# A gated mix of a state-space scan and a long convolution: every fourth step scanned, 32 x 64 conv digits, and half of the output gated first

## The chip, the cores and the metric

The kernel runs on one core of one Trainium2 chip. The metric is the device time of one execution in microseconds; the runs shown are three executions of the kernel before. Engines are named as in the profile: PE (TensorE, matmuls), PEld (its weight loads), DVE (VectorE), ACT (ScalarE), POOL (GpSimd), SP (SyncE, which here only issues DMAs). The 16 DMA engines are counted together.

## What is computed

Two sequence models read the same x (2048 steps, 1024 channels, bf16) and a sigmoid gate mixes them, one gate per step.

```python
def _A_ref(x, Lambda_re, Lambda_im, B_re, B_im, C_re, C_im, log_dt, Dskip):
    ...
    Lam_bar = jnp.exp(dt * Lam)
    B_bar = ((Lam_bar - 1.0) / Lam)[:, None] * Bmat
    Bu = jnp.einsum("bld,pd->blp", x + 0j, B_bar)
    for t in range(L):
        h = Lam_bar[None, :] * h + Bu[:, t, :]
        hs.append(h)
    y = 2.0 * jnp.einsum("blp,dp->bld", hseq, Cmat).real + x * Dskip[None, None, :]

def _B_ref(q, k, v, shift_k, ssm_k, ssm_D):
    # k_shift: a causal filter of 4 taps over k, per channel
    kv = k_shift * v
    # y: the causal convolution of kv with ssm_k over all 2048 steps, per channel, by FFT
    y = y + kv * ssm_D[None, None, :]
    return q * y

g = _sigmoid((x * gate_w).sum(-1, keepdims=True))
return g * _A_ref(x, ...) + (1 - g) * _B_ref(x, B_k, B_v, ...)
```

There are 1024 complex states. Matmuls take bf16 and accumulate in fp32.

## The kernel before, in words

**The planner.** The kernel does not issue its work in program order. Every piece of work is given to a `_Plan` by `op` (L76): its engine, an assumed duration, the tiles that it reads and writes, and a priority. `schedule` (L114) then simulates the engines with these durations, with the buffers in SBUF (21 slabs of 8 KB per partition), eight PSUM banks in pairs and a serial DMA server, and fixes the order on each engine; `emit` (L294) writes the instructions in that order. The priorities are the tables PS, PU, PO, PC, PH, PG. A piece with an `alt` may go to a second engine: evacuations from PSUM (`evac`, L519) to ACT or DVE, many DMAs to SP's queue or POOL's. Each queue is in order, so a waiting instruction holds what stands behind it.

**S5, the scan (L836 on).** States are taken 128 at a time, in 8 groups `pi`. x is loaded transposed (`load_x`, L612) in four tiles `xT` of 512 steps: odd and even steps, first and second half. `gemm_u` (L875) multiplies B and x, re and im apart, 16 matmuls of 128x128 by 512 for each tile. For even steps it adds the product of the previous odd step with the transition (`prev`, L885), so that only every second step has to be scanned. `rot` (L905) turns the input by the phase of the transition, scans re and im with the real decay (L923), and turns back: four DVE products and sums on each side; it does so for two chunks of 512, with a carry computed on POOL. `odd` (L943) then computes the odd steps from the even ones with 6 matmuls. Four of the eight groups stay in SBUF, four go to the scratch `h_scr` and come back.

**The convolution (L701 on).** Channels are taken 128 at a time, in 8 groups `u`. `kvprep` (L716) loads k and v transposed, applies the four taps and multiplies by v on DVE (some on ACT), and writes the product to `kv_scr`; `load_A` (L702) reads it and the kernel rows back with the time axis over the partitions in 16 parts of 128. The transform has digits 16, 16 and 16: `stage1` (L742), 8 matmuls of 128 columns; `spec` (L753), for two of 16 frequencies a matmul of 512 columns and two of 256; `product` (L766), the complex product, a DVE product of 2048 (L772) and two sums of 512 (L776); `inverse` (L780), matmuls of 256 and 128 columns, an evacuation and four DMAs that move one digit across partitions into `zb`; and `final` (L795), 8 full matmuls of 512, a multiplication by x on DVE (L808) and a DMA to the scratch `pB_scr`.

**The output (L1085).** Sixteen blocks of 256 steps by 512 channels: for each half 16 matmuls of 512 columns over all eight state groups (L1125). The conv part is read from `pB_scr`, scaled by 1 - g on ACT (L1107), x times Dskip is added on DVE (L1099, L1113), and a DVE operation adds g times the matmul's result (L1134). A block needs all state groups and its rows of `pB_scr`. The C matrices are combined with the coefficients of B on ACT and DVE before (L1053 to L1065). The gate's sums are matmuls on four column tiles (`gates`, L958).

The lines that the prediction names: L510 to L520 are helpers (`dma`, `evac`), so all DMAs show as L513 (transposing) or L515, and all evacuations as L520.

Of the kernel before, what the change touches and what calls it, by code (L numbers as in the profile page):

```python
# [15 lines left out]
MAGIC = 12582912.0  # L16
# [3 lines left out]


# [9 lines left out]
class _Op:  # L31
    __slots__ = ("alt", "eng", "dur", "fn", "prio", "n", "succ", "tiles", "alloc", "ready", "start", "end", "dma", "idx")


class _Plan:
# [3 lines left out]
    SLAB = 8192  # L39

    def __init__(self, nslab, nps):
        self.ops = []
        self.tags = {}
        self.nslab, self.nps = nslab, nps
        self.nbig, self.horizon, self.bias = 4, 40.0, 0.0
        self.least, self.spare = {}, 0

    def tile(self, tag, shape, dtype=BF16, cap=2, hold=False, loose=False):
# [4 lines left out]
        size = 2048 if b <= 2048 else 4096 if b <= 4096 else 8192  # L53
        assert b <= 8192
# [21 lines left out]
    def op(self, eng, dur, fn, r=(), w=(), prio=0.0, dma=None, alt=None):  # L76
        o = _Op()
        o.alt = alt
# [27 lines left out]
        for p_ in preds:  # L106
            p_.succ.append(o)
        for t in o.tiles:
            t.touches += 1
# [4 lines left out]
    def schedule(self, free0):  # L114
# [5 lines left out]
        halves = [[None] * 4 for _ in range(self.nslab)]  # L120
# [13 lines left out]
        def find(size, loose):  # L134
            k = size // 2048
            best = None
            big = sum(left[tg] + live.get(tg, 0) for tg, c_ in caps.items() if c_[1] == 8192 and not c_[3])
            for s, h in enumerate(halves):
                if big and (s < self.nbig) != (size == 8192 and not loose):
                    continue  # L140
                used = 4 - h.count(None)
                for q in range(0, 4, k):
                    if all(x is None for x in h[q:q + k]):
                        pair = (h[q ^ 1] is not None) if k == 1 else False
                        sc = (pair, used)
                        if best is None or sc > best[0]:
                            best = (sc, s, q)
            return best and best[1:]

        def fits_after(t):  # L150
            big = sum(left[tg] + live.get(tg, 0) for tg, c_ in caps.items() if c_[1] == 8192 and not c_[3])
            lo = self.nbig if big else 0
            free = sum(h.count(None) for h in halves[lo:]) - t.size // 2048
            need = 0
            for tg, (cap, size, hold, loose) in caps.items():
                if size and not hold and not loose and (size < 8192 or not big):
                    need += max(0, min(self.least.get(tg, 1), cap) - live.get(tg, 0)) * size // 2048 if left[tg] else 0
            return free >= need + self.spare

        def take(o):  # L160
            got = []
            for t in o.tiles:
# [9 lines left out]
                else:  # L172
                    if t.order != nexta.get(t.tag, 0) or live.get(t.tag, 0) >= t.cap or (t.hold and not fits_after(t)):
                        break
# [46 lines left out]
        while True:  # L221
            progress = True
            while progress:
                progress = False
                for e in engs:
# [3 lines left out]
                    for o in cand:  # L229
# [14 lines left out]
                        if o.dma is None:  # L244
                            o.end = now + o.dur
                            efree[e] = o.end
# [71 lines left out]
def kernel(  # L318
# [31 lines left out]
    SE = S // 2  # L350
    CW = 512
    NC = SE // CW
# [3 lines left out]
    NG = CH // 8  # L356
# [6 lines left out]
    kv_scr = dram.tile([D, S], BF16, name="kv_scr")  # L363
    h_scr = dram.tile([NP, NC, 128, 4 * CW], BF16, name="h_scr")
    g_scr = dram.tile([2, SE], F32, name="g_scr")

# [5 lines left out]
    prow = parm.tile([32, 128], BF16, name="prow")  # L372
    for i, v1d in enumerate((A_log_dt, A_Lambda_re, A_Lambda_im, A_Dskip)):
# [5 lines left out]
    sdz = parm.tile([128, D // 8], BF16, name="sdz")  # L379
    nc.vector.memset(sdz, 0.0)  # L380
# [4 lines left out]
    nc.vector.memset(mpi_col, -math.pi)  # L385
    mpih_col = consts.tile([128, 1], F32, name="mpih_col")
# [4 lines left out]
    make_identity(nc, ident)  # L391
    psum = ctx.enter_context(tc.tile_pool(name="psum", bufs=1, space=bass.MemoryType.PSUM))
# [5 lines left out]
    nc.tensor.matmul(psums[0][:, 0:32], lhsT=prow, rhs=ident[0:32, 0:32], start=True, stop=True)  # L398
    pcol = parm.tile([128, 32], F32, name="pcol")
    nc.vector.tensor_copy(pcol, psums[0][:, 0:32])  # L400
# [6 lines left out]
    dco = parm.tile([128, NP, 3], F32, name="dco")  # L407
# [24 lines left out]
    r2 = small("r2")  # L432
    mul(r2, rv, rv)
# [13 lines left out]
    TS(out=phn, in0=thn, scalar1=2.0, scalar2=None, op0=ALU.mult)  # L447
    rc = dco[:, :, 0]
    mul(rc, rv, cth)
    rs = dco[:, :, 2]  # L450
    mul(rs, rv, sth)
    mrs = dco[:, :, 1]
    TS(out=mrs, in0=rs, scalar1=-1.0, scalar2=None, op0=ALU.mult)
# [17 lines left out]
    phU = small("phU")  # L471
    TS(out=phU, in0=phn, scalar1=float(CW), scalar2=None, op0=ALU.mult)
    rqU = small("rqU")
    TS(out=rqU, in0=phU, scalar1=MAGIC, scalar2=-MAGIC, op0=ALU.add, op1=ALU.add)
    TT(out=phU, in0=phU, in1=rqU, op=ALU.subtract)
    sU = small("sU")
    nc.scalar.activation(out=sU, in_=phU, func=ACT.Sin, scale=TWO_PI)
    faU = small("faU")
    nc.scalar.activation(out=faU, in_=phU, func=ACT.Abs)
    cU = small("cU")  # L480
    nc.scalar.activation(out=cU, in_=faU, func=ACT.Sin, bias=pihalf_col, scale=-TWO_PI)
    sU2 = parm.tile([128, NP, 2], F32, name="sU2")
    TS(out=sU2[:, :, 0], in0=sU, scalar1=-1.0, scalar2=None, op0=ALU.mult)
    nc.vector.tensor_copy(sU2[:, :, 1], sU)
# [3 lines left out]
    omgc = parm.tile([128, 16], F32, name="omgc")  # L488
# [702 lines left out]
```

## Time and profile before

| | us |
|---|---|
| median of three runs | 434.52 (430.0 to 436.05) |
| span of the profiled execution | 427.0 |
| PE busy | 398.4 (93%) |
| DVE busy | 346.7 (81%) |
| ACT busy | 267.8 (63%) |
| POOL busy | 132.7 (31%) |
| packets of SP's DMA queue, share of 16 engines' span | 69.8% |
| packets of POOL's DMA queue | 16.9% |

The profile gives the span, from the first to the last instruction of one execution, and no other time of that execution; 434.52 - 427.0 = 7.5 us lie around it against the median. The DMA queues moved 71.87 MB in 153,596 packets, 129,861 of them under 512 bytes. Matmuls are pipelined: the mean of one (379 ns for 512 columns) is its way through the array and not the distance to the next; distances are read from the chain or the timeline, where a run of them stands with its count. DMA shares are sums of packet times and can exceed 1.

### The profile page before, as it was taken

Reading aid. Unit: us, or ns where it says so; the run is one execution under the profiler, and the core shown is the slowest. Engines: PE = TensorE matmul, PEld = TensorE weight load, DVE = VectorE, ACT = ScalarE, POOL = GpSimd, SP = SyncE. Lnnn points to the kernel's source line nnn. Section 1 sums busy time; section 2 is a strip of 40 time slices with the busy share of each in tenths; the row PEclk is TensorE's granted clock in tenths of the full one; section 3 lists DMA queues with packets and bytes.
Section 4 is the critical chain, followed back from the end, with each engine's and each line's share of the span. In section 5 each row is a group of like instructions: output and inputs, shape, how many; then the busy total and the mean of one; then the engine's idle time right before and its main releaser. Section 6 shows DMA issues by size and latency. Waiting matters only on the chain.

```text
span 427.0 us, 7194 instructions
## 1 busy us (share of the span) xinstructions
PE 398.4 (93%) x2691; PEld 228.5 (54%) x2736; DVE 346.7 (81%) x513; ACT 267.8 (63%) x310; POOL 132.7 (31%) x172
## 2 busy tenths in 40 slices
PE   7598999999999789999969999899989999999996
PEld 6353544655566456566635655676544444444442
DVE  4998999999979789989889989979696969724422
ACT  3489488747589679477966786999554286203100
POOL 6994611232464134753634403340010000000000
PEclk9999999999999999999998999999999999999999
DMA  8999999459999999598999369999989996405111
GB/s 149 113 196 195 194 232 231 174 90 160 158 186 193 256 217 185 127 207 173 187 184 164 90 192 166 287 184 178 174 163 185 213 234 205 143 22 177 49 37 62
DMA packets 153596, 71.87 MB, mean 168 GB/s; under 512 B 129861, under 2 KB 147541, under 8 KB 153561
## 3 DMA queue, kind: packets, MB, share of 16 engines
q1 hardware_dynamic: 146120, 54.55, 69.8%
q0 software_dynamic: 7360, 16.85, 16.9%
q8 instruction: 21, 0.34, 0.4%
q14 instruction: 15, 0.11, 0.1%
q10 hardware_dynamic: 80, 0.01, 0.0%
HBM read 24.93 MB, written 16.79 MB: 98 GB/s over the span
## 4 chain that ended last, share of the span: by engine, by line
PE 68%; DMA 11%; SPq 10%; ACT 4%; DVE 3%; issue 3%; POOL 0%; DVEq 0%; ACTq 0%; POOLq 0%
PE ps L1125 22%; PE ps L882 20%; SPq L513 8%; DMA slab<-slab 5%; PE ps L760 4%; ACT slab L520 4%; PE ps L747 4%; DMA slab<-in_A_x_dram 4%; PE ps L889 3%; PE ps L950 3%; DMA slab<-in_B_ssm_k_dram 3%; PE ps L761 2%; PE ps L786 2%; PE ps L762 2%; SPq L515 2%
## 5 line engine op out<-in xcount | busy, mean ns | idle before, releaser
L520 ACT CAST slab<-ps 128x1024 bf16<-128x1024 f32 x197 | 185.4, 1042 | 62.8 <-PE ps L892 17.6
L882 PE MATMUL ps<-slab,slab 128*128 128x512 bf16 (+1 forms) x527 | 115.8, 370 | 6.3 <-DMA slab<-in_A_B_re_dram 3.1
L1125 PE MATMUL ps<-slab,slab 128*128 128x512 bf16 x485 | 109.1, 379 | 1.0 <-DVE slab L1134 0.4
L882 PEld LDWEIGHTS <-slab 128*128 128x128 bf16 x544 | 52.8, 99 | 60.0 <-issue 5.5
L1125 PEld LDWEIGHTS <-slab 128*128 128x128 bf16 x512 | 49.8, 98 | 59.6 <-issue 0.7
L515 POOL DMA_DIRECT2D slab<-slab x84 | 51.4, 618 | 57.8 <-ACT slab L520 51.9
L1134 DVE SCALAR_TENSOR_TENSOR slab<-ps,gcols,slab 128x512 bf16<-128x512 f32 x32 | 23.6, 747 | 39.1 <-PE ps L1125 36.1
L1107 ACT ACTIVATE slab<-slab,omgc 128x512 bf16<-128x512 bf16 x32 | 21.2, 714 | 45.2 <-DMA slab<-pB_scr 40.1
L760 PE MATMUL ps<-slab,fC 128*128 128x512 bf16 x118 | 44.9, 381 | 1.1 <-ACT slab L520 0.6
L747 PE MATMUL ps<-tab,slab 128*128 128x128 bf16 x512 | 35.0, 222 | 7.5 <-POOL slab L712 6.2
L911 DVE TENSOR_TENSOR slab<-slab,slab 128x2048 bf16<-128x2048 bf16 x31 | 37.7, 1217 | 3.5 <-PE ps L747 1.5
L772 DVE TENSOR_TENSOR slab<-slab 128x2048 bf16<-128x2048 bf16 x32 | 38.6, 1215 | 1.8 <-ACT slab L520 1.5
L747 PEld LDWEIGHTS <-slab 128*128 128x128 bf16 x512 | 31.4, 99 | 12.3 <-POOL slab L712 6.8
L761 PE MATMUL ps<-slab,fS 128*128 128x256 bf16 x128 | 35.0, 273 | 0.6 <-issue 0.2
L762 PE MATMUL ps<-slab,fN 128*128 128x256 bf16 x128 | 35.0, 274 | 0.0
L786 PE MATMUL ps<-slab,gC 128*128 128x256 bf16 x128 | 29.9, 273 | 1.7 <-DVE slab L776 1.7
L776 DVE TENSOR_TENSOR slab<-slab 128x512 bf16<-128x512 bf16 x64 | 24.9, 416 | 6.3 <-PE ps L950 2.3
L788 PE MATMUL ps<-slab,gS 128*128 128x128 bf16 x128 | 28.0, 219 | 0.0
L787 PE MATMUL ps<-slab,gN 128*128 128x128 bf16 x128 | 28.0, 219 | 0.0
L735 DVE TENSOR_TENSOR slab<-slab,slab 128x2047 bf16<-128x2047 bf16 (+2 forms) x22 | 26.7, 1213 | 0.0
L808 DVE TENSOR_TENSOR slab<-ps,slab 128x1024 bf16<-128x1024 f32 x16 | 19.3, 1216 | 3.3 <-PE ps L806 2.8
L1113 DVE SCALAR_TENSOR_TENSOR slab<-slab,gcols,slab 128x512 bf16<-128x512 bf16 x26 | 18.3, 745 | 3.5 <-ACT slab L1107 3.4
(184 smaller groups left out, 532.5 us busy)
## 6 DMA issues: line engine op xcount, KB each, us to landing
slab<-in_A_x_dram SPq DMA_DIRECT2D x22, 256.0 KB
slab<-slab POOLq DMA_DIRECT2D x84, 64.0 KB, 5.3
slab<-h_scr SPq DMA_DIRECT2D x8, 512.0 KB
slab<-pB_scr SPq DMA_DIRECT2D x16, 256.0 KB
out_dram<-slab SPq DMA_DIRECT2D x15, 256.0 KB
slab<-in_B_ssm_k_dram SPq DMA_DIRECT2D x7, 512.0 KB
pB_scr<-slab SPq DMA_DIRECT2D x12, 256.0 KB
slab<-slab SPq DMA_DIRECT2D x44, 64.0 KB
```

Of the source, the lines that this page charges most:

```text
L513: nc.sync.dma_start_transpose(out=o_, in_=i_)
L515: QS[q].dma_start(out=o_, in_=i_)
L520: op("ACT", 1.04, lambda: A.copy(o_(), i_()), r=r, w=w, prio=prio, alt=("DVE", 1.2, lambda: V.tensor_copy(o_(), i_())))
L747: PE_.matmul(ps.ap[:, i, :], lhsT=a.ap[:, 8 * q + i, :], rhs=t1v[:, hh * 128:(hh + 1) * 128], start=True, stop=True)
L760: PE_.matmul(ps.ap[:, i], lhsT=fC[:, k2, :], rhs=zz, start=True, stop=False)
L761: PE_.matmul(ps.ap[:, i, :, 0, :], lhsT=fS[:, k2, :], rhs=zz[:, :, 1, :], start=False, stop=False)
L762: PE_.matmul(ps.ap[:, i, :, 1, :], lhsT=fN[:, k2, :], rhs=zz[:, :, 0, :], start=False, stop=True)
L772: TT(out=T.ap, in0=K.unsqueeze(2).to_broadcast([128, 2, 2, 4 * CH]), in1=W_.unsqueeze(1).to_broadcast([128, 2, 2, 4 * CH]), op=ALU.mult)
L786: PE_.matmul(ps.ap[:, i], lhsT=gC[:, k2, :], rhs=pp.ap[:, :, i, :], start=True, stop=False)
L882: PE_.matmul(ps.ap[:, ri, k0:k1], lhsT=BT.ap[:, d, ri, :], rhs=t.ap[:, d, k0:k1], start=(d == 0), stop=(par == 1 and d == ND - 1))
L911: TT(out=out, in0=tab.ap.unsqueeze(2).to_broadcast([128, 2, 2, CW]), in1=x.unsqueeze(1).to_broadcast([128, 2, 2, CW]), op=ALU.mult)
L1125: PE_.matmul(ps.ap, lhsT=Hr[pi, a // 4].ap[:, par, ri, (a % 4) * 128:(a % 4 + 1) * 128], rhs=CT[pi, dh][0].ap[:, CT[pi, dh][1], ri, :], st ...
```

## The change

**Scan.** re and im of 64 states are stacked in the 128 partitions of a tile, and only every fourth step is scanned. x comes in four tiles of 512 steps, by step modulo 4. The first three phases are plain products; the fourth (j = 0) adds the products of the three steps before it, on column tiles of 64. After the scan `step` computes first the state scaled by the coefficients of B (j = 0, on 64-row tiles) and then the three other phases, one from the other. C is used as it is loaded. As the tiles now hold halves, the two halves of each state group are exchanged through `h_scr`, also for the groups that stay in SBUF.

```diff
-        def gemm_u(BT, dg, Hc, par, c, pr, split=False):
+        def gemm_u(BT, dg, dp, H, j, pr):
...
+                    if j:
+                        PE_.matmul(ps.ap[:, k], lhsT=BT.ap[:, d, k].rearrange("p r c -> p (r c)"), rhs=t.ap[:, d], start=(d == 0), stop=(d == ND - 1))
+                    else:
+                        for h in range(2):
+                            PE_.matmul(ps.ap[64 * h:64 * h + 64, k], lhsT=BT.ap[:, d, h, k, :], rhs=t.ap[:, d], start=(d == 0), stop=False)
...
+        def step(dg, H, pi, j, pr):
+            ps = pl.psum([2, CW])
+
+            def f():
+                for k in range(2):
+                    for h in range(2):
+                        if j:
+                            PE_.matmul(ps.ap[:, h, :], lhsT=dg.ap[:, 4 * h + 2 - 2 * k:4 * h + 4 - 2 * k].rearrange("p o c -> p (o c)"),
+                                       rhs=H.ap[:, h, j - k, :], start=(k == 0), stop=(k == 1))
+                        else:
+                            PE_.matmul(ps.ap[:, h, :], lhsT=dg.ap[64 * h:64 * h + 64, 8 + 2 * k:10 + 2 * k].rearrange("p o c -> p (o c)"),
+                                       rhs=H.ap[64 * h:64 * h + 64, k, 0, :], start=(k == 0), stop=(k == 1))
```

**Convolution.** The digits are 32 (time in 32 parts of 64), 64 and 32. The trip of kv through `kv_scr` is replaced by a DVE transpose of 32x32 blocks. Kernel rows are read in pieces of 64 values. Stage 1 and the spectrum run on 64-row tiles. The complex product becomes one DVE product over a copy of the spectrum whose halves are exchanged (`turn`, two DMAs of 64 partitions), and the inverse adds the parts. The last stage runs in 32x32 tiles, with the factor 1 - g folded into its table and g x Dskip added by one-row matmuls.

```diff
+                V.transpose(t.ap.bitcast(F32).rearrange("p c w -> p w c"), src.ap.bitcast(F32).rearrange("p (n w) -> p w n", w=32))
...
+                    for t in range(2):
+                        PE_.matmul(ps.ap[:, t, i, :], lhsT=a.ap[64 * t:64 * t + 64, c:c + 2].rearrange("p g n -> p (g n)"),
+                                   rhs=t1v[64 * t:64 * t + 64], start=True, stop=True)
...
+                        for g in range(2):
+                            PE_.matmul(ps.ap[:, g, i, :], lhsT=tF[64 * g:64 * g + 64, k1, 64 - 64 * r:192 - 64 * r],
+                                       rhs=z.ap[64 * g:64 * g + 64, k1 % 16, r].rearrange("p w c -> p (w c)"),
+                                       start=(r == 0), stop=(r == 1))
...
+            def lo():
+                return [kv.ap[0:64, 2], kv.ap[64:128, 2]]
+
+            def hi():
+                return [kv.ap[64:128, 0], kv.ap[0:64, 0]]
+            dma("SP", 0.8, lo, hi, [(kv, 0), (kv, 1)], [(kv, 2)], pr, n=2, alt="POOL")
...
+                t = kv.ap[:, 0:3:2].rearrange("p b i c -> p b (i c)")
+                TT(out=t, in0=t, in1=kv.ap[:, 1].rearrange("p i c -> p (i c)").unsqueeze(1).to_broadcast([128, 2, 8 * CH]), op=ALU.mult)
...
+                        PE_.matmul(ps.ap[:, i], lhsT=tG[:, 8 * q + i, b, :], rhs=kv.ap[:, 2 * b, i, :], start=(b == 0), stop=(b == 1))
...
+                dma("SP", 0.65, lambda h=h: [zb.ap[8 * q + 4 * h + i:128:32].rearrange("s r n c -> s (r n) c") for i in range(4)],
+                    lambda h=h: [qq.ap[:, 4 * h + i] for i in range(4)], [qq], [(zb, (q, h))], pr, n=4, issue=0.6, alt="POOL", alt_issue=0.65)
...
+                for n in range(4):
+                    for q in range(4):
+                        PE_.matmul(ps[q // 2].ap[:, q % 2, n], lhsT=gl[32 * q:32 * q + 1, n, :], rhs=dsk.ap[32 * q:32 * q + 1, cs],
+                                   start=(n == 0), stop=False)
+                for n in range(4):
+                    for b in range(2):
+                        for e in range(4):
+                            for q in range(4):
+                                PE_.matmul(ps[q // 2].ap[32 * e:32 * e + 32, q % 2, n], lhsT=tabG[32 * q:32 * q + 32, b, 4 * n + e, :],
+                                           rhs=zb.ap[32 * q:32 * q + 32, b, 4 * n + e, :], start=False, stop=(n == 3 and b == 1),
+                                           tile_position=(32 * q, 32 * e))
```

**Output.** Blocks are 512 steps by 256 channels, in matmuls of 256 columns. Channels 512 to 1023 come first: their matmul results are scaled by g on ACT or DVE and written to a scratch `pA_scr`, without the conv part; the conv groups u = 4 to 7 later read that back, add it and write the output. For channels 0 to 511 the conv part is read from `pB_scr` and one DVE operation finishes it.

```diff
+            late = dq in DQS[:2]
...
+                if late:
+                    op("ACT", 0.34, lambda: A.activation(out=ot.ap[:, a, :], in_=ps.ap, func=ACT.Copy, scale=col(gcols, 4 * j + a)),
...
+            if late:
+                dma("SP", 0.9, lambda: [rows(pA_scr)], lambda: [ot.ap], [ot], [(e_pA, (dq, j))], prs[1] + 3)
...
+                    dma("SP", 2.6, parts(ga), rows(pA_v), [(e_pA, (u // 2, j)) for j in range(NF)], [ga], prx[1], n=4, alt="POOL", alt_issue=0.9)
+                    op("DVE", 1.23, lambda: TT(out=xs.ap, in0=xs.ap, in1=ga.ap, op=ALU.add), r=[ga, xs], w=[xs], prio=pr[1])
```

**Planner.** Slabs become 11 of 16 KB, tiles may have 6 and 16 KB, the planner charges 0.1 us (`SWITCH`) where PE's tile shape changes, ranks the tags when buffers are short, and all priorities and caps are new.

More of the change, by code (lines that the diff above doesn't have):

```diff
@@ L107, in op @@
             p_.succ.append(o)
+        for t in pre:
+            if t not in o.tiles:
+                o.tiles.append(t)
         for t in o.tiles:
@@ L469 @@
     TS(out=mc2r, in0=c2r, scalar1=-1.0, scalar2=None, op0=ALU.mult)
[L471 to L479, printed above, removed]
```

857 lines of the change are left out of this document (433 added, 424 removed), and 34 rows, old and new, of tables (PR, PS, PU).

## Prediction

> **What bounds the kernel now.** I read the page's totals first, then the busy time by stretch of the span, then the chain that ended last, then the groups by form.
>
> Page: busy time, and DMA share in 40 slices.
>
> ```profile
> PE 398.4 (93%) x2691; PEld 228.5 (54%) x2736; DVE 346.7 (81%) x513; ACT 267.8 (63%) x310; POOL 132.7 (31%) x172
> DMA  8999999459999999598999369999989996405111
> ```
>
> Windows, with busy time of PE, PEld, DVE, ACT, POOL, then PE clock, DMA share, GB/s.
>
> ```profile
> 0.00:37.00 37.00, 28.26 (x219) 18.50 (x222) 31.00 (x74) 22.48 (x31) 32.55 (x28) 0.95 1.12 148
> 10.00:331.00 321.00, 299.15 (x2175) 180.46 (x2209) 289.11 (x409) 238.72 (x269) 125.24 (x159) 0.99 0.99 182
> 247.75:250.00 2.25, 2.25 (x16) 1.19 (x14) 2.22 (x5) 1.08 (x2) 0.00 (x0) 1.00 0.38 99
> 252.00:254.00 2.00, 2.00 (x24) 1.41 (x23) 0.66 (x2) 1.72 (x2) 0.66 (x3) 1.00 0.98 383
> 331.00:370.00 39.00, 38.43 (x176) 17.40 (x178) 33.06 (x52) 20.43 (x28) 0.00 (x0) 1.00 0.91 217
> 370.00:427.00 57.00, 53.10 (x243) 23.97 (x245) 19.73 (x29) 5.34 (x8) 0.00 (x0) 0.99 0.20 65
> ```
>
> From 10 to 331 us three resources are full together: PE 93%, DVE 90%, DMA share 0.99 (shares above 1 occur, so 1 is no hard cap). From 370 us on only PE works: output matmuls alone. So the end is set by PE's sum of work plus the holes that late data leave.
>
> Chain that ended last (start us, us, what).
>
> ```profile
> 37.00 1.91 PE ps L964 x31
> ...
> 85.67 3.45 PE ps L882 x16
> ...
> 95.29 0.89 PE ps L747 x16
> ...
> 143.64 7.01 issue
> ...
> 212.17 11.65 DMA slab<-in_B_ssm_k_dram
> ...
> 423.40 0.75 DVE slab L1134
> ```
>
> A full 512-column matmul costs 3.45/16 = 0.2156 us, a 128-column one 0.89/16 = 0.0556; a 256-column one shows as 0.11 (0.108). Four 32-column tiles run beside each other: 31 of 512 columns in 1.91 us, 0.053 each once the last one's 0.38 is taken off. The two long holes are behind kernel-row loads (in_B_ssm_k), with DMA share 1.15 to 1.16 around them.
>
> PE's sum before, in 0.2156 units: input products 512, previous-step products 64, odd steps 96, output 512, conv last stage 64: 269. Gates 1.9; conv stage 1 512 x 0.0556 = 28.5; spectrum 128 x (0.2156+2 x 0.108) = 55.2; inverse 128 x (0.108+2 x 0.0556) = 28.1; warm-up 5. Total **388**, of a span of 427.0: 39 us of holes, namely 6 before 10 us, 7 while x arrives (10 to 37), some 22 up to 331, 4 at the end.
>
> **PE after, part by part.** Scan every 4th step with stacked re and im: three phases of input products stay full, 8 x 3 x 16 = 384 units; the fourth has 256 products on 128x64 tiles, two beside each other, 128. Previous-step products: 96, paired, 48. Steps: 8 x 3 x 4 = 96, and 32 of 64 rows, paired, 16. Sum 672 units, 144.9. Output: 1024 of 256 columns, 110.6. Gates 1.9. Conv stage 1: 512 of 128 columns on 64-row tiles, paired, 14.2. Spectrum: 1024 such, paired, 28.5. Inverse: 512 full ones of 128 columns, 28.5. Warm-up 4. That is 332.5 without the last stage.
>
> Is pairing real? Warm-up tiles of the trace (64x64 is L1010, 64x128 is L1014, then full):
>
> ```profile
> 8.76 0.43 PE L1010 MATMUL ps<-ident 64*64 64x128 bf16 x8
> 9.12 0.50 PE L1014 MATMUL ps<-ident 64*128 64x256 bf16 x6
> 9.55 0.62 PE L604 MATMUL ps<-dskd,ones 128*128 128x128 bf16 x8
> ```
>
> L1014: (0.50-0.27)/5 = 0.045 us against 0.108 unpaired, so yes. Spectrum and stage 1 need 0.028 per matmul; L1010 shows quartets 0.107 apart, 0.027 each. I cost pairs in full. Unpaired, the same parts would add 84.
>
> The last stage has no row: 128 matmuls of 32x32 and 16 of one row, for each of 8 channel groups. Lower bound: 16 beside each other (row tiles shown four ways), (8+4) x 0.0556 = 0.67. Upper: L1010's 0.027 for each of 144, 3.9. The nearest row is the upper one; I take 3.0, in sum 24 (5 to 31).
>
> By the Trainium skill, "TensorE: Matmul & The Clock Gate", section "Wait — 56ns, not 53.3ns?", starts of matmuls never come closer than about 25 ns however small they are; that would make the stage 3.6 and its sum 29, and speaks against tiles this small. L1010's 27 is near it, though a quartet then took 0.107, twice the 0.0556 of later 128-column matmuls.
>
> Changing tile shape drains the array: the last L1010 quartet starts at 8.87, L1014 at 9.12, 0.25 where 0.107 was due (0.14 lost); L1014 to L604 loses 0.10. I take 0.12. In the PE order of before, stage 1 and spectrum alternate with other work 94 times; with the last stage (16), column-tiled products (16) and first steps (some 14) 140 switches, 17 us (10 to 42, the latter with every group alone: 304 x 0.14). PE's sum: 332.5+24+17 = **373.5** (348 to 406), 14 less.
>
> **Vector and scalar work.** DVE before:
>
> ```profile
> L923 DVE TENSOR_TENSOR_SCAN slab<-r,wlp,slab 128x512 bf16<-128x512 f32 x16 | 19.6, 1266 | 0.0
> L776 DVE TENSOR_TENSOR slab<-slab 128x512 bf16<-128x512 bf16 x64 | 24.9, 416 | 6.3 <-PE ps L950 2.3 <-PE ps L788 2.3 <-DMA slab<-slab 1.7
> L712 POOL TENSOR_TENSOR slab<-slab,sdz 128x16 bf16<-128x16 bf16 x8 | 5.4, 670 | 19.4 <-DMA slab<-in_B_ssm_k_dram 10.5 <-PE ps L762 8.9
> L520 ACT CAST slab<-ps 128x1024 bf16<-128x1024 f32 x197 | 185.4, 1042 | 62.8 <-PE ps L892 17.6 <-PE ps L889 15.3 <-PE ps L882 12.4
> ```
>
> Rotations and scans halve: 8 fewer at 1.22+0.84+2.47+1.22+0.84 = 6.59, -52.7. L776 goes, -24.9. Of the output's work L1113, L1099, L1065, L1055, L1063 go, -50; L1134's 23.6 becomes 32 half-size ones, 15 (12 to 24). Added: 8 block transposes of 1024 32-bit words, no row; an fp32 operation of 512 takes 0.69, an int32 one of 2048 2.2, so 1.2 to 2.3 each, 2.2 taken, 18; four adds 5; larger diagonals 8. DVE 347 to about **242**. ACT: evacuations 208 to 224 (+17), stage 1's in two halves (+6), L1107, L1053, L1059 gone (-42), half the gating added (+11): **260**. Both drop well under PE, and no step of them ends on the path but the last multiply. If the cover went, DVE's 18 us of transposes would stand before stage 1; PE has S5 products to run meanwhile.
>
> **DMA.** Before: 86.7% of 427, that is 370 us of all 16 engines. Prices per MB in engine-us: transposes 16 x 1.12/0.148 = 121 (0 to 37 us); 4 KB rows 16 x 0.98/0.383 = 41 (252 to 254, state reloads); 512-byte digit moves 16 x 0.38/0.099 = 61 (247.75 to 250, those alone); 256-byte pieces from the remainder, (5930 - 21.2 x 121 - 12.6 x 41 - 20.7 x 61)/16.8 = 94. After: transposes 21.0 MB; kernel rows 4.2 in 128-byte pieces, 94 to 188, 156 taken (31, 24, so about 20 ns a packet); the new half swap of each spectrum 8.4 in 2 KB, 41 to 61, 50 taken; digits 8.4, now 256-byte; other 256-byte traffic 10.5; 512-byte 6.3; states 12.6. Sum 6290, **393 us** (372 to 408) against 370: the bytes are the same 71 MB, the pieces smaller. At the 0.99 of 10 to 331 us this alone needs 397 us, so DMA ends about with PE. DMA instructions go from some 300 to 600; at 0.59 (SP) and 0.62 (POOL) plus transposes they take some 420 us of two queues' 800.
>
> The half swap puts a DMA into each of 32 spectrum, swap, product, inverse chains. Behind it on SP stand loads and digit moves, for which the last stage waits; POOL landings have a median of 5.3 us. Other blocks cover it (27 such tiles may live), except in the last block: +5 at the end.
>
> **Holes.** Half of the output no longer needs the conv, so 55 us of matmuls can fill holes between 200 and 330 us, where now output starts at 310. The first input product now waits for both halves of its x tile, where it took them one by one; a half takes 2.6 us of SP's queue, nothing hides it, +2. Of 39 us I keep 13 at the start, 10 of 22 in the middle, and 5 at the end; with the 2 that is 30. Span 373.5+30 = 403.5, which DMA's 397 just allows. The gate's new rows and some 20 small DMAs are costed at nothing: the gate's sum left at 46.8 us before, and the first last stage came at 130.9; without that distance one such chain of two landings is 11 us. The median of the runs lies 434.52-427.0 = 7.5 above the profiled span (no other time of that execution is given): **411**.
>
> **Rivals.** (1) Tiles cheaper than my rows: last stage 0.67, switches 10: PE 348, DMA at 1.1 needs 357, span 348+30 = 378, time **385**. For: quartets and pairs in the trace; against: no 16-way row. (2) The gain is eaten by drains: all 304 switches at 0.14 and last stage at 3.9: 406+30 = 436, less the 5 at the end that a PE-bound order hides, 431, time **438**: no change to speak of. Against it: 94, not 256, alternations in the order of before. (3) Slower: the digit moves crowd few DMA engines. While 8-partition moves ran alone (247.75 to 250) the share never passed about half; now each move writes 4 partitions, so a quarter. 8.4 MB x 94 = 790 engine-us; if SP issues a third, as of 128 now (44), and always on the same four, these carry 263/4 = 66 of it, 33 of the other two thirds, and (6290-790)/16 = 344 of the rest: 443 at 0.99 gives 447, time **455**. It decides once SP's part exceeds a quarter. Against: shares of 1.2 to 1.36 were sustained. The Trainium skill, "DMA: Bandwidth & Descriptors", section "Why a DMA increments its semaphore by 16 and not by 1", says that a copy runs on as many engines as divide its slowest dimension, from SP the lowest-numbered; the half share agrees.
>
> **How the numbers follow.** My sum 0.52 (0.47 of it faster by over 2%, 0.05 within), (1) 0.25, (2) 0.09, (3) 0.14. Two per cent, 8.7 us, is about what a measurement of this kernel can tell from no change. Faster 0.72, same 0.14, slower 0.14. The sum's own range is 393 to 429; 380 to 440 leaves out (3) and the far part of (1).
>
> **What would show it.** Right: DVE near 242, ACT near 260, DMA's packet time 390 or more, output matmuls between conv blocks before 300 us, no DMA-free tail of 57 us. Wrong: pairs spaced 0.056 instead of 0.028, last stages far from 3 us, digit moves landing over 10 us, or PE waiting for swaps (DMA slab<-slab) for more than 20 us.

## The result and the profile after

The changed kernel took **561.3 us** (median of four runs, 558.94 to 565.1), the kernel before 432.26 (428.8 to 436.05): a ratio of 1.303, interval 1.292 to 1.314. Slower by 129 us, where 411 was forecast. The profiled execution took 563.64 with a span of 561.9.

Totals of the changed kernel's page, and its clock and DMA rows in 40 slices:

```profile
span 561.9 us, 12598 instructions
PE 395.5 (70%) x5195; PEld 274.3 (49%) x5216; DVE 287.6 (51%) x392; ACT 251.6 (45%) x325; POOL 189.6 (34%) x271
PEclk9966999999999569799576599789987888977969
DMA  6953984755879748789848999799989695997956
q1 hardware_dynamic: 147768, 49.29, 56.4%
q0 software_dynamic: 12080, 22.91, 25.0%
```

PE is busy for as long as before (398.4) but idle for 166 us instead of 29. Over the whole span no engine is near full, and DMA is not either: the two queues' packets took 81.4% of 561.9, 457 us of all 16 engines, where 370 were measured before. So the time is not bound by a sum of work: things wait for each other.

Windows (PE, PEld, DVE, ACT, POOL, clock, DMA share, GB/s) show where; the line that stands alone is the kernel before:

```profile
0.00:40.00 40.00, 19.62 (x150) 11.09 (x153) 11.19 (x67) 4.42 (x13) 10.49 (x17) 0.88 0.73 134
40.00:180.00 140.00, 125.78 (x1077) 61.59 (x1087) 126.97 (x156) 117.09 (x133) 48.33 (x58) 0.96 0.71 126
180.00:320.00 140.00, 68.36 (x1161) 44.70 (x1170) 53.69 (x59) 53.44 (x68) 43.21 (x67) 0.75 0.78 138
320.00:400.00 80.00, 68.47 (x1035) 61.44 (x1017) 40.32 (x40) 37.53 (x61) 35.65 (x52) 0.91 1.07 135
400.00:561.90 161.90, 113.30 (x1804) 95.50 (x1801) 55.45 (x72) 39.16 (x54) 51.87 (x78) 0.84 0.85 122
```

```profile
180.00:320.00 140.00, 130.24 (x1037) 84.00 (x1052) 122.75 (x179) 109.56 (x121) 47.45 (x71) 0.99 0.93 180
```

PE loses 20 us in the first 40, 72 us between 180 and 320, and 49 after 400. From 320 to 400 it loses 12, and there DMA is full as well (1.07). The view of the waits (engine, line, waited for: us in total, times, longest) names two kinds of DMA between SBUF tiles, and the filling of sco:

```profile
ACT slab L601 <- PE ps L842: 117.1, 20, 23.2
PE ps L842 <- DVE slab L832: 57.7, 6, 22.3
DVE slab L832 <- DMA slab<-slab: 53.8, 8, 16.3
PE ps L871 <- DMA slab<-slab: 19.4, 2, 15.2
DVE slab L935 <- DMA sco<-gl: 18.4, 1, 18.4
```

Read it from below: the diagonal (L935) waits for sco at the start; the last stage (L871) waits for digit moves; the product (L832) waits for the exchange of halves, the inverse (L842) for the product, and ACT's evacuation for the inverse.

The chain that ended last could be followed back only to 517 us. It shows SP's queue standing in front of digit moves:

```profile
526.65 2.68 SPq L596
529.38 1.39 SPq L596
530.80 2.70 SPq L596
...
538.45 0.53 SPq L596
539.02 0.53 SPq L596
...
542.16 2.91 DMA out_dram<-slab
545.08 1.54 PE ps L871 x127
546.62 11.84 PE ps L1180 x96
558.48 0.48 DVE slab L1189
```

Each SPq piece is SP issuing one DMA. It takes 0.53 us from 535 us on, and up to 2.70 just before, after POOL issued eight digit moves (521.6 to 527.0). The windows around it (columns as above) show packets that take long for few bytes: a share of 1.34 moves 79 GB/s, and with SP's moves alone 0.33 moves 57.

```profile
528.00:530.00 2.00, 2.00 (x21) 1.79 (x20) 0.48 (x1) 0.00 (x0) 0.00 (x0) 1.00 1.34 79
536.00:538.00 2.00, 0.00 (x0) 0.00 (x0) 0.00 (x0) 0.00 (x0) 0.00 (x0) 1.00 0.33 57
540.00:542.00 2.00, 0.00 (x0) 0.00 (x0) 0.00 (x0) 0.00 (x0) 0.00 (x0) 0.50 0.34 56
```

### The profile page after: what moved, and what is told of

Read it like the earlier page. It is cut to its first block, busy times and chain, and to the rows that moved or that the text cites. A ratio compares the mean times of both kernels' runs of the same rounds, so it can differ in the third digit from the quotient of the medians.

```text
span 561.9 us, 12598 instructions
## 1 busy us (share of the span) xinstructions
PE 395.5 (70%) x5195; PEld 274.3 (49%) x5216; DVE 287.6 (51%) x392; ACT 251.6 (45%) x325; POOL 189.6 (34%) x271
## 5 line engine op out<-in xcount | busy, mean ns | idle before, releaser
L601 ACT CAST slab<-ps 128x1024 bf16<-128x1024 f32 x136 | 132.1, 1031 | 176.3 <-PE ps L842 117.1
L596 POOL DMA_DIRECT2D slab<-slab x152 | 101.5, 674 | 177.8 <-ACT slab L601 106.2
L1180 PE MATMUL ps<-slab,slab 128*128 128x256 bf16 x960 | 121.5, 284 | 1.6 <-ACT slab L803 1.5
L842 PE MATMUL ps<-slab,tG 128*128 128x128 bf16 x512 | 41.4, 252 | 61.9 <-DVE slab L832 57.7
L842 PEld LDWEIGHTS <-tG 128*128 128x128 bf16 x512 | 38.4, 115 | 65.6 <-DVE slab L832 37.0
L832 DVE TENSOR_TENSOR slab<-slab 128x2048 bf16<-128x2048 bf16 x32 | 38.2, 1221 | 55.3 <-DMA slab<-slab 53.8
L803 ACT CAST slab<-ps 128x512 bf16<-128x512 f32 x96 | 49.6, 626 | 15.0 <-PE ps L792 15.0
L814 PE MATMUL ps<-slab,tF 64*128 64x128 bf16 x1024 | 35.9, 228 | 4.0 <-ACT slab L803 2.0
L871 PE MATMUL ps<-slab,tabG 32*32 32x128 bf16 x1024 | 12.3, 274 | 37.3 <-DMA slab<-slab 19.4
L814 PEld LDWEIGHTS <-tF 64*128 64x128 bf16 x1024 | 32.3, 101 | 8.7 <-issue 7.2
L601 DVE CAST slab<-ps 128x1024 bf16<-128x1024 f32 x24 | 28.8, 1218 | 14.6 <-ACT slab L601 9.0
L977 PE MATMUL ps<-slab,slab 128*64 128x512 bf16 x256 | 30.4, 381 | 1.4 <-DMA slab<-in_A_B_re_dram 0.8
L935 DVE TENSOR_TENSOR slab<-id,sco 128x512 bf16<-128x512 bf16 (+1 forms) x11 | 8.8, 801 | 42.2 <-DMA slab<-slab 23.8
L871 PEld LDWEIGHTS <-tabG 32*32 32x32 bf16 x1024 | 10.4, 95 | 39.5 <-issue 23.3
```

Of the source, the lines that this page charges most:

```text
L596: QS[q].dma_start(out=o_, in_=i_)
L601: op("ACT", 1.04, lambda: A.copy(o_(), i_()), r=r, w=w, prio=prio, alt=("DVE", 1.2, lambda: V.tensor_copy(o_(), i_())))
L803: return lambda: [fn(put(hh), get(hh)) for hh in range(2)]
L814: PE_.matmul(ps.ap[:, g, i, :], lhsT=tF[64 * g:64 * g + 64, k1, 64 - 64 * r:192 - 64 * r], rhs=z.ap[64 * g:64 * g + 64, k1 % 16, r].rearra ...
L832: TT(out=t, in0=t, in1=kv.ap[:, 1].rearrange("p i c -> p (i c)").unsqueeze(1).to_broadcast([128, 2, 8 * CH]), op=ALU.mult)
L842: PE_.matmul(ps.ap[:, i], lhsT=tG[:, 8 * q + i, b, :], rhs=kv.ap[:, 2 * b, i, :], start=(b == 0), stop=(b == 1))
```

## The experiments

Each is a single run; the kernel before, run beside them, took 427.8 to 433.7 us, so differences under some 6 us are not told apart. The code cuts show the arguments and lines that carry the edit; the expectation says what else it takes. Theories: A, the digit moves, now written to 4 partitions each, crowd few DMA engines; B, the exchange of halves; C, small pieces; D, the start.

**Digit moves spread (471).**

```diff
-lambda h=h: [zb.ap[8 * q + 4 * h + i:128:32].rearrange("s r n c -> s (r n) c") for i in range(4)]
+lambda h=h: [zb.ap.rearrange("p r n c -> p (r n) c")[:, 8 * q + 4 * h + i] for i in range(4)]
```

> The kernel after, with each digit move (128 pieces of 256 bytes) written to 128 partitions of its tile in place of 4; number, size, queue and order of all DMAs stay. It leaves out the change of digits itself, so the last stage works on data in another order. Theory A, the digit moves use only a quarter of the DMA engines and hold up their queues: the moves of SP's queue come out about 0.6 us apart in place of 1.2 to 2.0, no stretch is left with a DMA share near 0.25 while SP is busy with them, and the time falls from 561 to 440 to 490 us. Theory B, the exchange of halves between spectrum and product sets the pace: 540 to 561. Theory C, the pieces are simply small (256 and 128 bytes) and the sum of DMA work is too large: 545 to 561, as the pieces stay the same.

Measured: 470.93. As many bytes, pieces and DMAs, and 90 us less, in the range of A. The packets' time fell from 457 to 373 us (57.7% and 21.8% of 469.1). SP's groups of eight and more DMAs between tiles came 0.65 to 1.16 us a DMA apart, not at 0.6 throughout. The waits for moves and for the exchange fell together:

```profile
DVE slab L832 <- DMA slab<-slab: 31.0, 6, 13.7
PE ps L842 <- DVE slab L832: 20.0, 7, 12.9
PE ps L871 <- DMA slab<-slab: 5.6, 7, 2.2
```

**No exchange (520).**

```diff
-            dma("SP", 0.8, lo, hi, [(kv, 0), (kv, 1)], [(kv, 2)], pr, n=2, alt="POOL")
+            dma("SP", 0.8, lambda: [], lambda: [], [(kv, 0), (kv, 1)], [(kv, 2)], pr, n=2, alt="POOL")
...
```

> The kernel after without the exchange of halves: its 64 DMAs are not issued, and the product on DVE (same shape, same 1.22 us) takes the spectrum's second half twice. It leaves out the exchange, so products are those of other rows. Theory B, the exchange sets the pace: PE's 58 us of waits behind the product (L842 after L832) and DVE's 54 us behind the exchange go, and the time falls to 490 to 515 us. Theory A: the exchange is late mostly because its queue is held up by digit moves, whose share near 0.25 stays; 530 to 555 us. If the exchange is hidden: 555 to 561.

Measured: 520.15, 41 us less: more than A alone allows, less than B asked.

**sco from the scalar engine's queue (555).**

```diff
-            nc.sync.dma_start(out=sco[64 * k:64 * k + 64, :, h], in_=vab[64 * h:64 * h + 64, k])
+            nc.scalar.dma_start(out=sco[64 * k:64 * k + 64, :, h], in_=vab[64 * h:64 * h + 64, k])
```

> The kernel after with the four small DMAs that fill sco (L571) issued on the scalar engine's queue in place of SP's, where they stand behind the transposes of x. Nothing is left out. Theory D, the start is late because of them: DVE's diagonal (L935) no longer waits until 34 us, PE's hole of 15.8 us before 46 us shrinks to under 3, and the time falls by 10 to 16 us, to 545 to 551. Rival: the 12 us are given back, since DMA and the digit moves set the pace later: 557 to 562.

Measured: 555.29, 6 us less, which alone is at the edge of what a single run tells; PE's hole shrank from 15.8 us to 10.1, not under 3. In the trace of the changed kernel the four DMAs stand on SP behind the transposes of x (start, length, engine, idle before):

```profile
27.34 2.00 SPq L594 DMA_TRANSPOSE slab<-in_A_x_dram  x1
29.46 2.78 SPq L571 DMA_DIRECT2D sco<-gl  x4
33.91 0.96 DVE L935 TENSOR_TENSOR slab<-id,sco 128x768 bf16<-128x768 bf16 x1 [18.39 <-DMA sco<-gl]
45.95 2.29 PE L974 MATMUL ps<-slab,slab 128*128 128x512 bf16 x5 [15.80 <-ACT slab L601]
```

DVE's diagonal, next on its engine, waits 18 us for these DMAs of 20 KB, and with it all of DVE's tables, ACT behind them, and PE. In the run with the edit:

```profile
14.92 10.79 ACTq L571 DMA_DIRECT2D sco<-gl  x4
30.26 0.96 DVE L935 TENSOR_TENSOR slab<-id,sco 128x768 bf16<-128x768 bf16 x1 [15.05 <-DMA sco<-gl]
```

The issue now starts 14.5 us earlier, but takes 10.8 us in place of 2.8, and DVE still waits 15.0 us. So the place behind the transposes is the smaller part of this wait, 3.3 us of 18.4; what makes these DMAs slow was not tried.

**All digit moves on POOL's queue (581).** The moves' call gets a fixed queue in place of the plan's; the order stays.

> The kernel after with all 256 digit moves issued on POOL's queue in place of 132 on SP's and 124 on POOL's. Nothing is left out. Theory A in the form that it is SP's moves that always meet the same four engines: the stretches with a DMA share of 0.25 disappear, SP's queue is free, POOL's issue rises by 132 x 0.67 = 88 us to about 280, and the time falls to 470 to 530 us. If four partitions are slow from either queue: moves on POOL land after 10 us or more, and the time stays at 545 to 580, for POOL's queue then holds all of them. Theory B: 545 to 561. The Trainium skill, DMA: Bandwidth & Descriptors, section Why a DMA increments its semaphore by 16 and not by 1, says that on the GpSimd queue the engines are taken in turn and on SP's the lowest-numbered; by it the first of these comes out.

Measured: 580.99, in time the second case (1 us above its range), though the moves landed in a median of 6.6 us and not 10. POOL issues one of 32 KB every 0.68 us, was 278 us busy in place of 190, and what stands behind waits: the last stage (L871) 46.7 us for moves. The first case did not come, and with it not what the rule of the Trainium skill cited there would give; as POOL's queue became so much fuller, the run does not show which engines the moves met.

**16 and 8 partitions (474, 498).**

```diff
+[... [(8 * q + 4 * h + i) % 8:128:8, 8 * ((8 * q + 4 * h + i) // 8):8 * ((8 * q + 4 * h + i) // 8) + 8] for i in range(4)]   # 16 partitions
```

For 8 partitions 16 stands in place of 8.

> The kernel after with each digit move written to 16 partitions, 8 apart, 8 pieces of 256 bytes in each, in place of 4 partitions with 32 pieces; the rest as it is. It leaves out the change of digits itself. With 4 partitions the time was 561 us, with 128 it was 471. Theory A1, what counts is how many DMA engines a move gets, and 16 is all of them: 468 to 478 us, moves landing in 3 to 4 us. Theory A2, what counts is how many partitions are written, in inverse proportion: (1/16 - 1/128)/(1/4 - 1/128) = 0.23 of the 90 us, 485 to 497 us.

> The kernel after with each digit move written to 8 partitions, 16 apart, 16 pieces of 256 bytes in each, as many partitions as in the kernel before. It leaves out the change of digits itself. Theory A1, engines, cost as 1/k: (1/8 - 1/16)/(1/4 - 1/16) = 0.33 of the 90 us, 495 to 507 us, and where only the moves run the DMA share stands at 0.5. Theory A2, partitions: (1/8 - 1/128)/(1/4 - 1/128) = 0.48, 508 to 520 us. A threshold that only 4 partitions pass: 470 to 480 us.

Measured: 473.53 and 497.57. With 4, 8, 16 and 128 partitions the time is 561, 498, 474 and 471. Both times hit A1: the cost falls about as 1/k and ends at 16. This fits what the Trainium skill states ("DMA: Bandwidth & Descriptors", section "Why a DMA increments its semaphore by 16 and not by 1"): a DMA runs on the largest number of engines up to 16 that divides the slowest dimension of both its sides. But the shares forecast did not come: neither 0.5 for 8 partitions, nor an end of the stretches near 0.25 for 128. While SP's moves ran alone it was 0.17 to 0.26 with 8, 16 and 128 partitions, and 0.33 with 4; one window with 8:

```profile
472.00:474.00 2.00, 2.00 (x20) 1.80 (x19) 0.48 (x1) 0.00 (x0) 0.00 (x0) 1.00 0.23 49
```

So such a share does not count engines, and no view names them: that engines are what runs short, and not something on the side of the partitions written, is inferred from the times. Median landings (last number) on POOL's queue, 4 partitions, then 16:

```profile
slab<-slab POOLq DMA_DIRECT2D x124, 32.0 KB, 7.3
slab<-slab POOLq DMA_DIRECT2D x28, 128.0 KB, 8.0
```

```profile
slab<-slab POOLq DMA_DIRECT2D x124, 32.0 KB, 3.5
slab<-slab POOLq DMA_DIRECT2D x28, 128.0 KB, 6.5
```

**The kernel before with its moves cut in two.**

```diff
-[zb.ap[4 * q + i:128:16].rearrange("s g r c -> s g (r c)") for i in range(4)]
+[zb.ap[64 * t + 4 * q + i:64 * t + 64:16].rearrange("s g r c -> s g (r c)") for i in range(4) for t in range(2)]   # 4 partitions
+[zb.ap[4 * q + i:128:16, :, r].rearrange("s g c -> s g c") for i in range(4) for r in range(2)]                     # 8 partitions
```

> The kernel before with each digit move (8 partitions written, 128 pieces of 512 bytes) cut in two that write 4 partitions each (64 pieces of 512 bytes); all else, order included, as before; nothing is left out. Theory A: in this kernel too four partitions hold up SP's and POOL's queues; PE waits, and the time goes from 431 to 470 to 530 us. Rival, that only the order of the kernel after makes them costly: 425 to 445 us. Its control, with as many moves of as many bytes, is the run that cuts them the other way.

> The kernel before with each digit move cut in two that write 8 partitions each (128 pieces of 256 bytes): 256 moves of 32 KB, as in the other cut, but twice the pieces. Nothing is left out. Theory A: it stays within 430 to 460 us, at least 30 us below the cut into 4 partitions, though it has twice the pieces. Rival, that the number of moves on the queues costs: both cuts come out alike. Rival, that small pieces cost: this one is the slower.

Measured: 460.26 and 466.23, against 427.97. The expectations of A failed: the cut into 4 is below its range of 470 to 530 (and above the rival's 425 to 445), and the cut into 8 is 6 us above the cut into 4 and not 30 below. What came is the rival of the second text: the number of moves costs, and both cuts come out alike within what a single run tells. POOL, which issues 168 of the 256 moves, rose from 132.7 us busy to 183.6 and 180.7. So in this kernel four partitions are not shown to cost more than eight. One reading saves A: if a move gets as many engines as partitions, either cut gives 16 pieces an engine (64/4, 128/8). It was not tried, and the number of moves on the queues explains both times without it.

**All three edits (440), without the exchange's (461), with kernel rows in 4 KB pieces (436); those pieces alone (549).**

```diff
-        src = B_ssm_k[u * CH:(u + 1) * CH, :].rearrange("(q c) (n m) -> q n c m", q=4, m=64)
+        src = B_ssm_k[u * CH:(u + 1) * CH, :].rearrange("(q n) (c m) -> q n c m", q=4, m=64)
```

> The kernel after with three edits at once: digit moves to 128 partitions (471 us alone), no exchange of halves (520 alone), sco filled from the scalar engine's queue (555 alone). It leaves out the change of digits and the exchange. If these three are the whole loss against the forecast of 411 us and add up: 561 - 90 - 41 - 6 = 424; 415 to 435 us, PE's holes 40 to 50 us. If the exchange was late mostly because of the digit moves, the two gains overlap: 440 to 460 us. If a third cause stays (PE's lower granted clock, K rows of 128-byte pieces, the order): above 460.

> The kernel after with spread moves and sco from the scalar engine's queue, the exchange kept. It leaves out the change of digits. If the exchange is late by itself: near 464 us (471 less 6), so 24 us above the run without exchange (440). If it was only late behind the moves and sco: 440 to 450 us.

> The kernel after with the kernel rows read in pieces of 4 KB in place of 128 bytes (same bytes, same 32 partitions a DMA); it leaves out the right order of the rows. Theory C, small pieces make the sum of DMA work too large: 4.2 MB at 156 less 41 engine-us a MB is 30 us of 16 engines, and the time falls by 15 to 30 us, to 531 to 546. Theory A, the engines that the digit moves crowd set the pace and these DMAs use all: 552 to 562.

> The run with spread moves, no exchange and sco from the scalar engine's queue (440 us), and kernel rows in 4 KB pieces besides. It leaves out the change of digits, the exchange and the order of the kernel rows. If these pieces still load DMA where it is the limit: their 12 us of alone come again, 425 to 432 us. If DMA has room by then (its shares are 0.5 to 0.9 from 300 us on): 436 to 441, and what remains above the forecast is holes of the order itself.

Measured: 439.62, 460.62, 548.87 and 436.45. From the changed kernel down: moves 561 to 471, sco to 461, exchange to 440, rows to 436. The 440 is at the lower edge of the case in which the gains overlap; PE's holes were 60 us, not 40 to 50. The exchange is worth 41 us alone and 21 (24 expected) once the moves are out of its way: about half of its loss was theirs, half its own. The rows' 12 us alone lie between the ranges of C and A, though their packet time fell by 27 us (457 to 430), near the 30 forecast; the last 3 are not told from none. Page totals and windows of the 436 us run:

```profile
PE 381.7 (88%) x5216; PEld 262.9 (60%) x5216; DVE 285.9 (66%) x392; ACT 250.6 (58%) x325; POOL 148.5 (34%) x243
0.00:40.00 40.00, 21.74 (x152) 11.52 (x153) 13.51 (x74) 4.80 (x14) 11.32 (x17) 0.88 0.83 134
40.00:200.00 160.00, 149.15 (x1428) 75.36 (x1431) 142.05 (x169) 131.03 (x145) 53.29 (x72) 0.97 0.67 137
200.00:280.00 80.00, 67.97 (x1098) 51.73 (x1087) 57.08 (x60) 47.55 (x67) 30.60 (x56) 0.91 0.93 189
```

**Which queue, which engines.** All moves on SP's queue, 4 or 16 partitions; then 4 partitions for one queue's moves only.

> The kernel after with all 256 digit moves (4 partitions) on SP's queue. Nothing is left out. Theory A1, moves from SP always meet the same four engines: 256 moves of 32 pieces an engine; SP's moves were 1.2 to 2.0 us apart when these engines were full, so SP's queue is held for 300 to 500 us, and the time rises to 600 to 720 us. If only their number on a queue counts (0.6 us each, 154 us in all): 540 to 580.

> As the run with all digit moves on SP's queue, but each written to 16 partitions. It leaves out the change of digits. Theory A1: SP issues them every 0.6 us, 79 us more of SP's queue than in the run with 16 partitions on both queues (474 us), partly beside other work: 475 to 520 us, at least 100 us below the run with 4 partitions. If their number on the queue counts: both runs come out within 30 us of each other.

> The kernel after with SP's 132 digit moves written to 16 partitions and POOL's 124 to 4; it leaves out the change of digits itself. 474 us with 16 partitions on both, 561 with 4 on both. If POOL's moves do the harm: 540 to 561. If SP's do: 474 to 490. If it takes both, meeting in the same engines: 480 to 500 here and in the other run, and the two gains over 474 add up to clearly less than 87 us. If they only add: the two losses sum to 87.

> The kernel after with SP's 132 digit moves written to 4 partitions and POOL's 124 to 16; it leaves out the change of digits itself. If POOL's moves do the harm: 474 to 495. If SP's do: 540 to 561. If it takes both: 480 to 500 here as in the other run. By the run with all moves on SP's queue (37 us for 256 moves), half as many give 19 us: 493.

Measured: 564.39, 527.04, 501.13 and 495.14. Both texts on SP's queue failed in A1: the time is not 600 to 720 us, and 37 us lie between the two runs, not 100 (nor under 30). With 16 partitions, all moves on SP's queue cost 53.5 us over both queues (474): in an order planned for two queues, the number of moves on one costs by itself. That SP's narrow moves hold its queue for 300 us is wrong; whether they always meet in the same four engines stays open. SP alone, in the run with all moves on its queue, issues 32 of them without a stop, 0.60 us each; the changed kernel takes 0.96 each for 16 where POOL's are in flight (start, length):

```profile
523.40 19.12 SPq L596 DMA_DIRECT2D slab<-slab  x32
```

```profile
525.98 15.29 SPq L596 DMA_DIRECT2D slab<-slab  x16
```

Groups of eight moves and more take 0.58 to 0.95 us a move there, 0.60 to 1.79 in the changed kernel, and 0.63 to 1.19 with 16 partitions on both queues. Narrow moves on one queue cost 28 (POOL's) or 22 us (SP's) over 474; on both, 88. (The kernel before ran 1.3% longer beside these two runs, so the 28 and 22 are if anything too large.) This is the case in which it takes both, 1 us above its range in one run: the two losses sum to 49 us, and some 38 us come only with narrow moves on both queues. That they slow each other is seen in two places. SP's 168 DMAs between tiles took 195 us to issue with both narrow, 143 and 148 with only POOL's or only SP's, 141 with neither (added up from the timelines). And POOL's narrow moves land in 7.3 us beside narrow ones from SP, in 5.4 beside wide ones:

```profile
slab<-slab POOLq DMA_DIRECT2D x124, 32.0 KB, 5.4
```

On which engines they meet, no view records; nor is it excluded that slack in the order hides part of either loss alone.

**Two remedies that leave nothing out (480, 470).** Digits through a scratch in device memory, one wide write and a late wide read; then also the exchange as two DVE copies of 64 partitions.

```diff
+out, src = [d_scr[u][8 * q:8 * q + 8].rearrange("i p c -> p i c")], [qq.ap]
+if zb.left == 0:
+    out += [zb.ap[32 * s:32 * s + 32].rearrange("k r n c -> k (r n c)") for s in range(4)]
+    src += [d_scr[u][:, 32 * s:32 * s + 32].rearrange("k m c -> k (m c)") for s in range(4)]
```

> The kernel after with the digits moved through a scratch in device memory: each result of the inverse is written from 128 partitions in 256-byte pieces (1 DMA in place of 8), and the last of four is followed by four reads of 32 partitions in pieces of 8 KB; 64 DMAs in place of 256, 8.4 MB more traffic; sco is filled from the scalar engine's queue. Nothing is left out. Theory A: all engines share it, so it comes near the run with spread moves, 470 less 6 us, plus up to 21 us for 8.4 MB at 41 engine-us a MB: 460 to 490 us. If two landings in a row before each last stage, and a queue that waits between them, cost as much as the crowding did: 510 to 560.

> As the run with the digits through a scratch, and the exchange of halves done by two copies of 64 partitions on DVE in place of two DMAs (32 pairs, about 0.4 us a copy by the 0.42 us that a 128x512 product took before: 26 us more of DVE, at 287). Nothing is left out. Theory B in its share of 41 us: 425 to 455 us, near the run without exchange and with spread moves. If DVE's order holds it up (copies stand before scans and evacuations): 460 to 490 us.

Measured: 480.40, as A asked, and 469.91, in the second case. DVE rose by 27.6 us to 315.2, as worked out, but POOL's waits for ACT before scratch writes rose from 47.1 to 65.5 us:

```profile
POOL d_scr L597 <- ACT slab L602: 65.5, 9, 20.5
```

Neither run comes near the kernel before.

## Why the prediction was wrong

- **The step that failed is the term for holes, 30 us, in the sum that gave 411.** The sum lets digit moves, exchange and sco cost PE's path nothing but 5 us at the end. PE was idle for 166 us. Taking out the waits for narrow moves, exchange, sco and kernel rows gave 125 us of time back, 90 of them by the moves alone.
- **Crowded moves stood beside the sum as rival (3), priced 455 and given 0.14.** That moves to few partitions cost is right, and the largest part; the way and the price are not. It took a third of the moves for SP, and half were SP's (132 of 256), but with half its own working gives only some 480 (99 + 25 + 344 at 0.99, and 7.5). It added packet time to four engines and divided; packet time did grow, from 373 to 457 us, but SP also stood at its DMAs, in the chain at the end for up to 2.7 us each, and loads and exchanges stand on the same queue. And it charged an average over the span, where the chain spectrum, exchange, product, inverse, moves, last stage pays each wait in turn. "Always on the same four" is shown neither way. The low share while moves run alone, which it took as agreeing with the rule that it cites, is no count of engines: it was no higher with 128 partitions than with 8.
- **"The half swap: +5 at the end."** 21 to 41 us measured. Its cover, 27 live tiles and other blocks, did not help: PE's order is fixed, and PE waited in place for L842 (57.7 us).
- **sco was not costed at all**: "some 20 small DMAs are costed at nothing". DVE's first work of the scan waits 18 us for it, and 15 when it has another queue; the other queue was worth 6 to 10 us, the first at the edge of what a single run tells. The rest of this wait is in the holes that remain.
- **Kernel rows in 128-byte pieces**: 30 us of packet time were put into the sum; 27 us of packet time and 12 us of time were measured alone, 3 us or none with the rest gone.
- **DMA's 393 us** (372 to 408) met 373 with spread moves, but 457 in the changed kernel, out of its range. "DMA ends about with PE" was not what bound it: its mean share was 0.82.
- **The queues: 420 us of two queues' 800.** SP alone stood issuing for 454 us in the changed kernel and 366 with spread moves, against 289 before (added up from the timelines): its queue was far fuller than an even split.
- **PE's sum held.** 381.7 busy in the 436 us run against 373.5, with the granted clock below 1 around holes (busy time lay 10 us above the sum in the kernel before too, 398.4 against 388). The last stage, 24 us in the sum, took 12.3 + 4.3 = 16.6, on the favourable side:

```profile
L871 PE MATMUL ps<-slab,tabG 32*32 32x128 bf16 x1024 | 12.3, 274 | 37.3 <-DMA slab<-slab 19.4
L865 PE MATMUL ps<-slab,gl 1*128 1x128 bf16 x128 | 4.3, 259 | 10.0 <-DVE slab L803 9.8
L814 PE MATMUL ps<-slab,tF 64*128 64x128 bf16 x1024 | 35.9, 228 | 4.0 <-ACT slab L803 2.0
L747 DVE STREAM_TRANSPOSE slab<-slab 128x1024 f32<-128x1024 f32 x8 | 16.7, 2087 | 1.2 <-PE ps L842 1.2
```

  Of L871's 32x32 matmuls 127 take 1.54 us at a granted clock of 0.50, 12 ns each; in the 436 us run 128 take 1.27 us at 1.00, 10 ns each. So the 25 ns floor of the Trainium skill ("TensorE: Matmul & The Clock Gate", section "Wait — 56ns, not 53.3ns?"), which would have made the stage 3.6 us a block, does not hold for tiles side by side. What the Trainium skill states on the same page, section "Part 3: Packing small matmuls — row/col tiling", some 4 ns a tile, is off on the other side. The spectrum's pairs came at 35.9/1024 = 0.035 us, part of them at a lower clock, not unpaired at 0.056. Block transposes took 2.09 us against 2.2. Where the tiles could gain, they did, and it did not decide the time. (The gates' 0.053 us is 0.051 by its own row, (1.91 - 0.38)/30; nothing hangs on it.)
- **DVE 287.6 against 242, ACT 251.6 against 260**: I put all evacuations on ACT; the plan gave DVE 49 us of them. At ACT's own means these 56 are 45 us, so the work put on ACT was 296 us and not 260, a miscount of its own. With DVE 51% busy and ACT 45%, neither set the pace.
- **What is left of the holes.** With the four causes out, 53 us against 30: 18 in the first 40 us (13 forecast) and 12 from 200 to 280. That is 23 of the 25 us still above 411; PE's 8 more are the rest, less 6, since executions lie 1.7 us above their own span and not 7.5: 436.45 - 434.7. What would close these last holes was not tried.
- **The signs to watch**: "PE waiting for swaps more than 20 us" and "DVE near 242" told of the miss; "digit moves landing over 10 us" did not, the median being 7.3 on POOL's queue, and "packet time 390 or more" came as a sign of being right. Output matmuls, forecast before 300 us, began only at 323.7 here, at 256.8 in the 436 us run.

## What to carry to other kernels

Before a DMA is cut or reshaped, count the partitions that it writes and the moves that it adds to a queue. Here 256 moves of 32 KB to 4 partitions each cost 88 us more than the same bytes to 16, most of it with such moves on two queues; with 16 partitions, all of them on SP's queue cost 53.5 us more than on two queues; and in the kernel before, cutting 128 moves into 256 cost 32 to 38 us, with 4 partitions or with 8. Price a DMA that enters a chain of dependent steps by its landing time in the kernel's own crowd, not by its packets' share; and when a DMA is added, write down what stands ahead of it on its queue. A sum of work in which each engine fits, as here with PE at 70% and DMA at 0.82, does not settle the end once the order on each engine is fixed.

## What the runs showed that was not expected

- Two queues sending narrow moves hurt more than both apart: 22 and 28 us alone, 88 together, and SP's issue of its 168 DMAs between tiles takes 195 us with both, 143 and 148 with one.
- In the chain at the end, one DMA issue on SP lasted up to 2.70 us after narrow moves from POOL, and 0.53 some microseconds later.
- POOL's own issue is dearer for narrow moves: its DMAs between tiles have a median of 0.69 us with 4 partitions, 0.59 with 8, 0.53 with 16 and 128.
- Sixteen partitions are as good as 128 (474 and 471 us), 8 are 24 us above that, 4 are 88 above.
- Tiles of 32x32 started 10 to 12 ns apart.
- PE's holes lower its granted clock too: in the hole from 535 us on it is 1.00 from 536 to 538 and 0.50 from 540 to 542. From 180 to 320 us it is 0.75 in the changed kernel, 0.99 before. PE's busy time is 395.5 us with the holes and 381.7 without most of them.
